# Maxima over two key blocks at once: key differences and relu beside the projections of a two-layer attention and MLP kernel

## The chip, the cores and the metric

The kernel runs on one core of one Trainium2 chip. Its time is what the device takes for one execution, in microseconds (us). The engines of the core work side by side: PE (TensorE) multiplies matrices, DVE (VectorE) and ACT (ScalarE) work on rows of up to 128 partitions, POOL (GpSimd) does the same more slowly and not on PSUM, SP (SyncE) issues DMAs. Each engine runs its own list of instructions in order and waits on the others by semaphores.

## The reference

Two layers, each an attention block and an MLP, on 2048 rows of 640 in fp32:

```python
x = x + _A_ref(_layernorm(x), wqkv, wo)      # 32 heads of 20
x = x + _B_ref(_layernorm(x), w1, b1, w2, b2) # 1536 wide, relu squared
x = x + _A_ref(_layernorm(x), wqkv, wo)
x = x + _B_ref(_layernorm(x), w1, b1, w2, b2)
# _A_ref: q, k, v = heads of x @ wqkv
scores = jnp.einsum("bhqd,bhkd->bhqk", q, k) * (Dh ** -0.5)
p = _softmax(scores, axis=-1)
o = jnp.einsum("bhqk,bhkd->bhqd", p, v)
```

The softmax needs the largest score of every query of every head over all 2048 keys. The kernel computes the scores twice: once with the queries on the partitions, only to take the maxima along the free axis, and once with the keys on the partitions, for the exponentials and the product with v. The negated maxima enter the second product as two more rows of q (against rows of ones in k).

## The kernel before

**Sizes.** Heads go in 8 groups of 4 (`g`), queries in 4 blocks of 512 (`qb`), keys in 4 blocks of 512 (`c`). A block of the attention is `t = 4 g + qb`, 32 in a layer. Matrices are kept as a rounded part and a remainder (`hi`, `lo`), and a product is taken as three.

**A pair.** For one `t`, one key block `c`, one of two head pairs `p` and one 128-row part `sub` of the queries, two matmuls of 60 rows by 512 columns (L434, `by_queries`, one for each head of the pair) give the scores, and DVE takes the maximum of each row. There are 32 × 4 × 8 = 1024 pairs in a layer. The maxima of a `t` lie in one small tile `mx` (`maxima`, 14 buffers), four numbers (one for each `c`) for each head and `sub`; `mrows_max` takes the largest of the four.

**Projections** (`qkv`). 40 units of 15 matmuls (`proj_unit`, L305) give q and k, 16 units of 30 (`v_unit`, L333) give v. The first 16 units make the first two of five row blocks of q and k for all four column blocks `tb`. A unit's result is split on ACT and POOL (`split_on_pool`) or ACT and DVE (`split_to`) and stored to DRAM by SP one unit later (`later`); keys and queries come back from DRAM as tiles of 512 columns, six DMAs each (`rows_of_heads`). After every projection matmul `between` adds 1 (0.65 for v) to a pace, and whenever it reaches 11, `some` issues three pairs (`smax_two`: one L455 reduction over two banks for the two heads). Their results go through three pairs of PSUM banks in turn (`ps_q`). The list of key blocks to work on is `EARLY`: what the finished column blocks allow of group 0, then group 1. The tiles of the next entry are loaded when an entry begins (`tiles`). Key tiles stay in SBUF for later use in `kept`, twelve of them. When all four key blocks of `t = 0` are done, its maxima are turned into rows.

**Attention.** Its order is written out as strings (`ORDERS`): a, b are scores for the exponentials (L502, then ACT's L509), m, n are maxima of the remaining pairs, one head each (L434, then DVE's L446, three banks in turn), V is the product with v of one block of 128 keys for four heads (L514). One string is a turn: 8 V, 32 scores, 12 to 16 pairs. `pairs` picks the string by due time: the remaining pairs, divided over the turns that remain until their block is needed. Finished blocks are divided by their sums on POOL (L558, L569), which waits for DMAs that spread the sums. `begin` loads queries, keys (two groups ahead) and v, and in layer 0 prepares weights on POOL.

**Buffers.** 42 slots of 4 KB a partition (`slot`) hold keys, queries, projections, exponentials and weights; 11 `x` tiles (`xtile`) hold rows, raw weights and the intermediate of the split. A buffer freed in the program goes to the next that asks, who waits until its last reader is done.

Of the kernel before, what the change touches and what calls it, by code (L numbers as in the profile page):

```python
# [28 lines left out]
SLOT = 1024  # L29
HALF = D // 2  # L30
EPS = 1e-5
SCALE = DH ** -0.5
NBLK = NG * NQB
NSLOT = 42
# [4 lines left out]
def tile_layers(  # L39
# [26 lines left out]
    def slot(shape, dtype, label):  # L66
        return arena.tile(shape, dtype, tag="slot", name=name(label))

    def dma(eng, dst, src):

        if dst.dtype == F32R:
            dst = dst.bitcast(F32)
        if src.dtype == F32R:
            src = src.bitcast(F32)
        eng.dma_start(dst, src)  # L75

    def xtile(label):
        return xpool.tile([P, D], F32, tag="x", name=name(label))
# [158 lines left out]
            sp.put(raw, k * 4, k * 4 + 2, 2, eng_hi, eng_lo)  # L237

    d_qk = dram.tile([2, 2, D, S], F32R, name="d_qk")
    d_v = dram.tile([S, H, 32], F32, name="d_v")  # L240
    d_o = dram.tile([D, NQB, 2 * QB], F32R, name="d_o")
    d_one = dram.tile([2, 2, QB], F32R, name="d_one")
# [22 lines left out]
        nc.scalar.copy(dst_hi, src)  # L265
        nc.vector.tensor_sub(dst_lo, src, dst_hi.bitcast(F32))  # L266

    def split_on_pool(dst_hi, dst_lo, src):

        r = xtile("r")[:, :QB]  # L270
        nc.scalar.copy(r, src)  # L271
        pool_hi(dst_hi, r)
        pool_lo(dst_lo, r, dst_hi.bitcast(F32))
# [21 lines left out]


    ORDER = [5, 0, 6, 1, 7, 2, 8, 3, 9, 4]
    xt_ = {}

    def proj_unit(pos, tb, between):  # L300
        dst = ps_pj("pj")
        n = 0
        for k in range(KD):
            for hw, hx in THREE:
                nc.tensor.matmul(  # L305
                    dst,
                    w_qk.piece(pos * 10 + hw * KD + k),
                    xt_[tb][k][:, hx, :],
                    start=(n == 0),
                    stop=(n == 3 * KD - 1),  # L310
                )
                n += 1
                between()
        ev = slot([P, 2, QB], F32R, "ev")
        (split_on_pool if tb or pos > 3 else split_to)(ev[:, 0, :], ev[:, 1, :], dst)
        which, jj = divmod(ORDER[pos], 5)
        return lambda: dma(
            nc.sync,
            d_qk[which, :, jj * P : (jj + 1) * P, tb * QB : (tb + 1) * QB].rearrange(
                "h p t -> p h t"  # L320
            ),
            ev,
        )

    def v_unit(tt, between):
        tb, i = divmod(tt, 4)
# [59 lines left out]
    QSEG = ((0, 0), (DH, 1), (2 * DH, 0))  # L386
    KSEG = ((0, 0), (DH, 0), (2 * DH, 1))

    def rows_of_heads(dst, which, segs, g, b):
        for par in range(2):  # L390
            for off, hl in segs:
                r0 = 64 * par + off
                src = d_qk[which, hl, 4 * g * DH : (4 * g + 4) * DH, b * QB : (b + 1) * QB]
                src = src.rearrange("(a b d) t -> b d a t", a=2, b=2)[par]
                dma(nc.sync, dst[r0 : r0 + DH], src)

    def load_k(g, c, keep):

        if not keep:
            k = slot([P, 2, QB], F32R, "k")  # L400
        elif (g % 3, c) in kept:
            k = kept[g % 3, c]
        else:
            k = kept[g % 3, c] = slot([P, 2, QB], F32R, "k")
# [3 lines left out]
        rows_of_heads(k, 1, KSEG, g, c)  # L408

    def load_q(t):  # L410
        g, qb = divmod(t, NQB)
        q_t[t] = slot([P, 2, QB], F32R, "q")
        rows_of_heads(q_t[t], 0, QSEG, g, qb)

    def load_v(g, c):
        v = slot([P, 8, 4 * 32], F32, "vg")
# [33 lines left out]
    def smax_two(t, p, sub, c):  # L450

        dst = ps_q.two()
        for par in range(2):
            by_queries(dst[:, par, :], t, p, sub, c, par)
        nc.vector.tensor_reduce(  # L455
            maxima(t)[:, 2 * p : 2 * p + 2, sub, c], dst, axis=AX.X, op=ALU.max
        )

    PAIRS = [(p, sub) for p in range(2) for sub in range(4)]

# [121 lines left out]
    def prep_job():  # L582
# [25 lines left out]
    def qkv(first, x_src, rest):  # L608

        pending, groups, work = [], [], []  # L610
        left.update((t, 4) for t in range(NBLK))
        done.clear()
        state = {"pace": 0, "n": 0}
        early, late = {}, {}

        def at(when, n, f):
            when.setdefault(n, []).append(f)
# [30 lines left out]

        def tiles(x):
            g, qb, c = x  # L650
            if (g, c) not in k_t:
                load_k(g, c, True)
            if g * NQB + qb not in q_t:
                load_q(g * NQB + qb)

        def end_group(x):
            g, qb, c = x
            t = g * NQB + qb
            left[t] -= 1
            if left[t]:  # L660
                return
            if t < 1:
                mrows_max(t)
                mrows(t)
                work.append(lambda: mrows_load(t))
            elif t > 2:
                del q_t[t]

        def some(n=3):
            for _ in range(n):  # L670
                if not work:
                    if not groups:
                        return
                    x = groups.pop(0)
                    tiles(x)
                    if groups:
                        tiles(groups[0])
                    work.extend((x, p, sub) for p, sub in PAIRS)
                w = work.pop(0)
                if callable(w):  # L680
                    w()
                    continue
                (g, qb, c), p, sub = w
                smax_two(g * NQB + qb, p, sub, c)
                done.add((g * NQB + qb, p, sub, c))
                if (p, sub) == PAIRS[-1]:
                    end_group(w[0])

        def between(cost):
            state["pace"] += cost  # L690
            if state["pace"] >= 11:
                state["pace"] -= 11
                some()
            state["n"] += 1
            if state["n"] % 4 == 0:
                next(rest, None)

        for n, (tb, pos) in enumerate(UNITS):
            while tb not in xt_:
                next(rest)  # L700
            run(early, n)
            later(proj_unit(pos, tb, lambda: between(1)))
            run(late, n)
            if pos == FIRST - 2:
                tiles(EARLY[tb][0])
            if pos == FIRST - 1:
                groups.extend(EARLY[tb])
            if first:
                w_qk.save_full(1)
                w_v.save_full(1)  # L710
            if pos >= FIRST and tb == NQB - 1 or n == 4 * FIRST - 1:
                w_qk.past(pos * 10 + 9, w_qk.got)
        for tt in range(NKT):
            later(v_unit(tt, lambda: between(0.65)))
            if first:
                w_v.save_full(1)
            if tt % 4 == 3:
                del xt_[tt // 4]
            if tt == 10:
                load_v(0, 0)  # L720
        w_v.drop()
        w_qk.drop()
        later()
        load_v(0, 1)
        while callable((work or [0])[0]):
            some(1)

# [11 lines left out]
    def attention(first, x_src, first_rows):  # L739
# [25 lines left out]
        def begin(i):  # L765

            t, u = divmod(i, NKT)
            g, qb = divmod(t, NQB)
            if u == 1:
                q_t.pop(t - 1, None)  # L770
                if t + 2 < NBLK and t + 2 not in q_t:
                    load_q(t + 2)
            if u % 4 == 1 and qb == 0:
                k_t.pop((g - 1, u // 4), None)
                for h in (1, 2):
                    if g + h < NG and (g + h, u // 4) not in k_t:
                        load_k(g + h, u // 4, True)
                if g and g + 2 >= NG:
                    del kept[(g - 1) % 3, u // 4]
# [12 lines left out]
            if i in split:  # L792
                split.pop(i)()
# [290 lines left out]
```

## Time and profile before

| what | us |
|---|---|
| median of three runs | 3791.23 |
| lowest and highest | 3785.96, 3791.42 |
| profiled execution | 3787.99 |
| its span | 3786.2 |
| projections, layer 0 (18.0 to 335.0) | 317.0 |
| attention, layer 0 (first to last product with v) | 1143.4 |
| projections, layer 1 (1918.0 to 2217.0) | 299.0 |
| attention, layer 1 | 1140.7 |

The profile is one execution. A group's row has the line, the engine, the operation, what it writes and reads with the shape, and its count; behind the bar stand the busy time, the mean in ns of one, and the engine's idle time just before them with what ended it. In a row of windows each engine has its busy time and, in brackets, its count of instructions within the stretch. The chain is the sequence of work that ended last, followed back from the end. P·V matmuls (L514) leave two records each.

### The profile page before, as it was taken

What the parts mean: (1) busy time and instruction counts of PE and PEld (TensorE: products, weight loads), DVE (VectorE), ACT (ScalarE), POOL (GpSimd) and SP (SyncE); (2) the same over time, 40 slices, a digit from 0 to 9 for tenths busy, and PEclk for the clock granted to TensorE, in tenths of its full rate; (3) what the DMA queues carried; (4) which work ended last, traced back from release to release, by engine and by line L of the source; (5) the groups of instructions that cost most, each with busy time, mean ns of one, the idle gap of its engine ahead of it and who ended that gap; (6) DMA issues with size and microseconds to landing.
All of it is one profiled execution on the core that took longest, in us unless ns stands there. A gap on an engine that the chain in (4) does not pass through costs nothing.

```text
span 3786.2 us, 62901 instructions
## 1 busy us (share of the span) xinstructions
PE 3738.8 (99%) x23572; PEld 2135.2 (56%) x23572; DVE 2931.4 (77%) x4500; ACT 2386.3 (63%) x4599; POOL 797.7 (21%) x889
## 2 busy tenths in 40 slices
PE   7999999999999999999999999999999999999999
PEld 5676343444443345988876754444444444369998
DVE  7999999999999993444469999999999999924443
ACT  2114999999999996122211159999999999951221
POOL 5430343211112111111143201211111121201110
PEclk9999999999999999999999999999999999999999
DMA  6553454322121125611244422222232211355111
GB/s 192 176 189 107 135 146 148 108 74 74 48 73 43 35 89 183 239 42 42 89 147 154 166 90 59 67 76 53 65 82 53 60 41 43 102 196 205 42 43 42
DMA packets 243433, 380.81 MB, mean 101 GB/s; under 512 B 65148, under 2 KB 111996, under 8 KB 243128
## 3 DMA queue, kind: packets, MB, share of 16 engines
q1 hardware_dynamic: 242584, 375.08, 32.0%
q8 instruction: 186, 3.05, 0.3%
q10 hardware_dynamic: 544, 1.71, 0.2%
q14 instruction: 119, 0.97, 0.1%
HBM read 244.05 MB, written 132.62 MB: 99 GB/s over the span
## 4 chain that ended last, share of the span: by engine, by line
PE 94%; DVE 3%; DMA 1%; ACT 1%; SPq 0%; issue 0%; POOL 0%; ACTq 0%; DVEq 0%; POOLq 0%
PE banks L514 27%; PE banks L294 20%; PE banks L502 18%; PE banks L434 18%; PE banks L305 6%; PE banks L333 4%; DVE mx L446 1%; DMA k<-d_qk 1%; SPq L75 0%; DVE mx L455 0%; PE banks L914 0%; DMA q<-d_qk 0%; DVE h L266 0%; DVE r L938 0%; ACT e L509 0%
## 5 line engine op out<-in xcount | busy, mean ns | idle before, releaser
L509 ACT ACTIVATE e<-banks 128x512 f32<-128x512 f32 x4096 | 2109.6, 617 | 158.0 <-PE banks L502 96.1
L446 DVE TENSOR_REDUCE mx<-banks 128x1 f32<-128x512 f32 x3204 | 1996.4, 683 | 183.7 <-PE banks L434 134.3
L434 PE MATMUL banks<-k,q 60*128 60x512 f32 x4096 | 1207.6, 443 | 10.8 <-DMA q<-d_qk 8.3
L502 PE MATMUL banks<-q,k 62*128 62x512 f32 x4096 | 1175.4, 430 | 3.1 <-ACT e L509 1.7
L514 PE MATMUL banks<-e,vg 128*32 128x512 f32 x8192 | 1093.0, 605 | 0.0
L434 PEld LDWEIGHTS banks<-k,q 60*128 60x128 f32 x4096 | 578.5, 184 | 636.1 <-DVE mx L446 501.6
L502 PEld LDWEIGHTS banks<-q,k 62*128 62x128 f32 x4096 | 613.8, 185 | 479.9 <-ACT e L509 446.9
L455 DVE TENSOR_REDUCE mx<-banks 128x2 f32<-128x1024 f32 x446 | 518.7, 1220 | 48.9 <-PE banks L434 36.3
L294 PE MATMUL banks<-w,h 128*128 128x320 f32 x2304 | 352.8, 312 | 2.9 <-DVE h L266 2.7
L514 PEld LDWEIGHTS banks<-e,vg 128*32 128x32 f32 x8192 | 161.6, 108 | 341.5 <-issue 319.5
L294 PEld LDWEIGHTS banks<-w,h 128*128 128x128 f32 x2304 | 340.9, 189 | 12.5 <-DVE h L266 6.9
L294 PE MATMUL banks<-xnT,w 128*128 128x512 f32 x1440 | 330.2, 390 | 0.0
L305 PE MATMUL banks<-xnT,wqk 128*128 128x512 f32 x1200 | 309.4, 404 | 0.2 <-DVE ev L266 0.2
L937 ACT ACTIVATE r<-banks,b_t 128x512 f32<-128x512 f32 x96 | 66.1, 688 | 374.9 <-PE banks L294 373.7
L294 PEld LDWEIGHTS banks<-xnT,w 128*128 128x128 f32 x1440 | 269.5, 188 | 55.2
L271 ACT COPY r<-banks 128x512 f32<-128x512 f32 x92 | 53.5, 587 | 341.6 <-PE banks L305 298.6
L305 PEld LDWEIGHTS banks<-xnT,wqk 128*128 128x128 f32 x1200 | 218.4, 190 | 68.7 <-issue 23.7
L558 POOL TENSOR_TENSOR few<-few,minus_t 128x16 f32<-128x16 f32 x62 | 179.9, 2902 | 304.4 <-DMA few<-d_s 299.5
L276 POOL CAST mr<-nt 128x32 fp32r<-128x32 f32 x64 | 13.5, 211 | 976.5 <-DVE nt L474 976.5
L957 DVE TENSOR_TENSOR x<-banks,x 128x320 f32<-128x320 f32 x128 | 62.8, 491 | 200.8 <-PE banks L294 191.5
L569 POOL TENSOR_TENSOR o<-o 128x512 f32<-128x512 f32 x62 | 79.6, 1284 | 553.0 <-PE banks L502 146.3
L938 DVE TENSOR_TENSOR r<-r 128x512 f32<-128x512 f32 x96 | 79.7, 830 | 132.0 <-ACT r L937 131.7
(61 smaller groups left out, 1673.4 us busy)
## 6 DMA issues: line engine op xcount, KB each, us to landing
q<-d_qk SPq DMA_DIRECT2D x636, 80.0 KB
d_qk<-ev SPq DMA_DIRECT2D x80, 512.0 KB
k<-d_qk SPq DMA_DIRECT2D x384, 80.0 KB
x<-d_x SPq DMA_DIRECT2D x96, 320.0 KB
d_o<-ot SPq DMA_DIRECT2D x248, 80.0 KB
ot<-d_o SPq DMA_DIRECT2D x38, 512.0 KB
d_v<-v SPq DMA_DIRECT2D x32, 512.0 KB
vg<-d_v SPq DMA_DIRECT2D x32, 512.0 KB
```

The lines of the kernel that those rows point to most:

```text
L294: nc.tensor.matmul(dst, a, b, start=(n == 0), stop=(n == last))
L305: nc.tensor.matmul(dst, w_qk.piece(pos * 10 + hw * KD + k), xt_[tb][k][:, hx, :], start=(n == 0), stop=(n == 3 * KD - 1),)
L333: nc.tensor.matmul(dst[:, :HALF], xt_[tb][k][:, hx, i * P : (i + 1) * P], w_v.piece(k * 4 + hw * 2 + hf), start=(j == 0), stop=(j == 3 * K ...
L434: nc.tensor.matmul(dst, q_t[t][b : b + 60, p, sub * P : (sub + 1) * P], k_t[t // NQB, c][b : b + 60, p, :], start=True, stop=True,)
L446: nc.vector.tensor_reduce(maxima(t)[:, 2 * p + par, sub, c : c + 1], dst, axis=AX.X, op=ALU.max)
L455: nc.vector.tensor_reduce(maxima(t)[:, 2 * p : 2 * p + 2, sub, c], dst, axis=AX.X, op=ALU.max)
L502: nc.tensor.matmul(dst, k_t[t // NQB, kt // 4][b : b + 62, p, (kt % 4) * P : (kt % 4 + 1) * P], q_t[t][b : b + 62, p, :], start=True, stop ...
L509: nc.scalar.activation(es[p][:, par, :], dst, AF.Exp, scale=SCALE)
L514: nc.tensor.matmul(acc[32 * h : 32 * h + 32, :], v_t[t // NQB, kt // 8][:, kt % 8, 32 * h : 32 * h + 32], es[p][:, par, :], start=(kt == 0 ...
L558: nc.gpsimd.tensor_tensor(few, few, minus_t, op=ALU.pow)
L569: nc.gpsimd.tensor_mul(o[:, 0, :], o[:, 0, :], o[:, 1, :])
L938: nc.vector.tensor_mul(r, r, r)
```

## The change

The maximum over two key blocks A and B is taken at once: with the difference of the keys, D = kB − kA, max(q·kA, q·kB) = q·kA + relu(q·D). So two key blocks still need two matmuls a head, but DVE has one pass over 512 numbers in place of two.

- `proj_unit`: where the unit makes the first two row blocks of k, the copy of even column blocks is kept in a tile `kf`; at odd ones POOL subtracts, splits the difference, and SP stores it to `d_kd`. These eight units always split on POOL.
- `step_two` multiplies with a difference tile and applies relu on ACT into two `x` tiles; `both_two`, one call of `some` later, multiplies with the even block and adds, reduces and stores the maximum in one `tensor_tensor_reduce` a head (two DVE instructions: the pass, and the read of its accumulator). Only columns 0 and 2 of the four are written; so every `mx` tile is first set to −3e38 by POOL.
- 16 of the 128 combinations of group, query block and key block (groups 0 and 1, `qb` 2 and 3, all four `c`) go this way: `DOUBLE`, eight entries, filled in at unit 16. `EARLY` keeps `qb` 0 and 1 of groups 0 and 1 and gains those of group 2.
- `some` runs at a pace of 8.6: three plain pairs, or, while `DOUBLE` lasts, one `both_two`, one plain pair, one `step_two`.
- Sixteen key tiles are kept, and attention loads keys three groups ahead. Keys 1 to 3 of group 0 are dropped when their maxima are done and loaded again beside the v units.

In all, 292 pairs are done beside the projections (128 of them as 64 doubled ones) and 732 in attention.

```diff
-    def rows_of_heads(dst, which, segs, g, b):
+    def rows_of_heads(dst, src_of, segs, g):
...
+    def load_kd(g, x):
+        k_t[g, x] = slot([P, 2, QB], F32R, "kd")
+        rows_of_heads(k_t[g, x], d_kd["de".index(x)], KSEG, g)
...
             mx_t[t] = small.tile([P, 4, 4, 4], F32, tag="mx", bufs=14, name=name("mx"))
+            nc.gpsimd.memset(mx_t[t], LEAST)
...
+        if which and pos < FIRST:
+            if tb % 2 == 0 and jj == 0:
+                keys["of"] = slot([P, 2, QB], F32, "kf")
+            kf = keys["of"][:, jj, :]
+            r = xtile("r")[:, :QB] if tb % 2 else kf
+            split_on_pool(ev[:, 0, :], ev[:, 1, :], dst, r)
+            if tb % 2:
+                kd = slot([P, 2, QB], F32R, "kd")
+                nc.gpsimd.tensor_sub(kf, r, kf)
+                pool_hi(kd[:, 0, :], kf)
+                pool_lo(kd[:, 1, :], kf, kd[:, 0, :].bitcast(F32))
...
+    def step_two(t, p, sub, x):
+        dst = ps_q.two()
+        res = [xtile("rl")[:, :QB] for _ in range(2)]
+        for par in range(2):
+            by_queries(dst[:, par, :], t, p, sub, x, par)
+        for par in range(2):
+            nc.scalar.activation(res[par], dst[:, par, :], AF.Relu)
+        return res
+
+    def both_two(t, p, sub, x, r):
+        dst = ps_q.two()
+        c = 2 * "de".index(x)
+        for par in range(2):
+            by_queries(dst[:, par, :], t, p, sub, c, par)
+        for par in range(2):
+            nc.vector.tensor_tensor_reduce(
+                out=r[par], in0=dst[:, par, :], in1=r[par],
+                scale=1.0, scalar=LEAST, op0=ALU.add, op1=ALU.max,
+                accum_out=maxima(t)[:, 2 * p + par, sub, c : c + 1],
+            )
...
-        [(0, qb, c) for qb in range(NQB) for c in range(NQB) if max(qb, c) == tb]
+        [(0, qb, c) for qb in range(2) for c in range(NQB) if max(qb, c) == tb]
...
-    EARLY[-1] += [(1, qb, c) for qb in range(NQB) for c in range(NQB)]
+    EARLY[-1] += [(1, qb, c) for qb in range(2) for c in range(NQB) if qb + c]
+    EARLY[-1] += [(2, qb, c) for qb in range(2) for c in range(NQB)]
+    DOUBLE = [(g, qb, x) for g in range(2) for qb in (2, 3) for x in "de"]
...
+        def some():
+            while later_rows:
+                mrows_load(later_rows.pop())
+            if not (begun or double or twos):
+                for _ in range(3):
+                    one()
+                return
+            if begun:
+                w, r = begun.pop()
+                (g, qb, x), p, sub = w
+                t = g * NQB + qb
+                both_two(t, p, sub, x, r)
...
+            one()
+            w = following(double, twos)
+            if w:
+                (g, qb, x), p, sub = w
+                begun.append((w, step_two(g * NQB + qb, p, sub, x)))
+            else:
+                one()
...
-            if state["pace"] >= 11:
-                state["pace"] -= 11
+            if state["pace"] >= 8.6:
+                state["pace"] -= 8.6
                 some()
...
+            if n == FIRST + 1:
+                groups.append((1, 0, 0))
+            if n == NQB * FIRST:
+                double.extend(DOUBLE)
...
-                for h in (1, 2):
+                for h in (0, 1, 2, 3):
                     if g + h < NG and (g + h, u // 4) not in k_t:
                         load_k(g + h, u // 4, True)
```

More of the change, by code (lines that the diff above doesn't have):

```diff
@@ L297, in tile_layers @@
     ORDER = [5, 0, 6, 1, 7, 2, 8, 3, 9, 4]
-    xt_ = {}
+    xt_, keys = {}, {}
     def proj_unit(pos, tb, between):
@@ L314, in proj_unit, with store @@
         ev = slot([P, 2, QB], F32R, "ev")
-        (split_on_pool if tb or pos > 3 else split_to)(ev[:, 0, :], ev[:, 1, :], dst)
         which, jj = divmod(ORDER[pos], 5)
[L317 to L323, printed above, removed]
+        rows = slice(jj * P, (jj + 1) * P)
+        kd = None
+        if which and pos < FIRST:
[9 more added lines that the diff above has]
+                pool_lo(kd[:, 1, :], kf, kd[:, 0, :].bitcast(F32))
+                if jj:
+                    del keys["of"]
+        else:
+            (split_on_pool if tb or pos > 3 else split_to)(ev[:, 0, :], ev[:, 1, :], dst)
+        def store():
+            cols = slice(tb * QB, (tb + 1) * QB)
+            dma(nc.sync, d_qk[which, :, rows, cols].rearrange("h p t -> p h t"), ev)
+            if kd is not None:
+                dma(nc.sync, d_kd[tb // 2, :, rows].rearrange("h p t -> p h t"), kd)
+        return store
     def v_unit(tt, between):
@@ L392, in rows_of_heads @@
                 r0 = 64 * par + off
-                src = d_qk[which, hl, 4 * g * DH : (4 * g + 4) * DH, b * QB : (b + 1) * QB]
+                src = src_of[hl, 4 * g * DH : (4 * g + 4) * DH]
                 src = src.rearrange("(a b d) t -> b d a t", a=2, b=2)[par]
@@ L400, in load_k @@
             k = slot([P, 2, QB], F32R, "k")
[L401 to L402 removed]
+        elif (g % 4, c) in kept:
+            k = kept[g % 4, c]
         else:
[L404 removed]
+            k = kept[g % 4, c] = slot([P, 2, QB], F32R, "k")
             for par in range(2):
@@ L407, in load_k @@
         k_t[g, c] = k
-        rows_of_heads(k, 1, KSEG, g, c)
+        rows_of_heads(k, d_qk[1, :, :, c * QB : (c + 1) * QB], KSEG, g)
     def load_q(t):
@@ L457, in smax_two @@
         )
+    def step_two(t, p, sub, x):
[13 more added lines that the diff above has]
+            nc.vector.tensor_tensor_reduce(
+                out=r[par],
+                in0=dst[:, par, :],
+                in1=r[par],
+                scale=1.0,
+                scalar=LEAST,
+                op0=ALU.add,
+                op1=ALU.max,
+                accum_out=maxima(t)[:, 2 * p + par, sub, c : c + 1],
+            )
     PAIRS = [(p, sub) for p in range(2) for sub in range(4)]
@@ L613, in qkv @@
         state = {"pace": 0, "n": 0}
-        early, late = {}, {}
+        early, late, later_rows, ended = {}, {}, [], set()
         def at(when, n, f):
@@ L650, in tiles @@
             g, qb, c = x
-            if (g, c) not in k_t:
-                load_k(g, c, True)
+            for c in [c] if c in range(4) else [c, 2 * "de".index(c)]:
+                if (g, c) not in k_t:
+                    if c in range(4):
+                        load_k(g, c, True)
+                    else:
+                        load_kd(g, c)
             if g * NQB + qb not in q_t:
@@ L658, in end_group, with following, one @@
             t = g * NQB + qb
[L659 to L666, printed above, removed]
-                del q_t[t]
[L669 to L682, printed above, removed]
+            ended.add(x)
+            rest = groups + double
+            if t > 1 and all(y[:2] != (g, qb) for y in rest):
+                del q_t[t]
+            if c not in range(4) and all(y[0] != g or y[2] != c for y in rest):
+                del k_t[g, c]
+            if (
+                g == 0
+                and (0, 2, "d") in ended
+                and all(y[0] for y in rest)
+                and not any(w[0][0] == 0 for w in work + twos + begun)
+            ):
+                for c in range(1, 4):
+                    del k_t[0, c], kept[0, c]
+            if t == 0:
+                left[t] -= 1
+                if left[t] == 0:
+                    mrows_max(t)
+                    mrows(t)
+                    later_rows.append(t)
+        def following(todo, queue):
+            if not queue:
+                if not todo:
+                    return None
+                x = todo.pop(0)
+                tiles(x)
+                if todo:
+                    tiles(todo[0])
+                queue.extend((x, p, sub) for p, sub in PAIRS)
+            return queue.pop(0)
+        def one():
+            w = following(groups, work)
+            if w:
                 (g, qb, c), p, sub = w
@@ L720, in qkv @@
                 load_v(0, 0)
+            if tt == 12:
+                for c in range(4):
+                    if (0, c) not in k_t:
+                        load_k(0, c, True)
         w_v.drop()
@@ L724, in qkv @@
         load_v(0, 1)
-        while callable((work or [0])[0]):
-            some(1)
+        for g, x in [y for y in k_t if y[1] not in range(4)]:
+            del k_t[g, x]
+        assert 0 in done
     ORDERS = {
```

20 lines of the change are left out of this document (15 added, 5 removed).

## The prediction

> **What bounds the kernel now.** I read the page first: engine totals, the slices, the chain that ended last, the costliest groups.
>
> ```profile
> span 3786.2 us, 62901 instructions
> PE 3738.8 (99%) x23572; PEld 2135.2 (56%) x23572; DVE 2931.4 (77%) x4500; ACT 2386.3 (63%) x4599; POOL 797.7 (21%) x889
> PE 94%; DVE 3%; DMA 1%; ACT 1%; SPq 0%; issue 0%; POOL 0%; ACTq 0%; DVEq 0%; POOLq 0%
> L509 ACT ACTIVATE e<-banks 128x512 f32<-128x512 f32 x4096 | 2109.6, 617 | 158.0 <-PE banks L502 96.1
> L446 DVE TENSOR_REDUCE mx<-banks 128x1 f32<-128x512 f32 x3204 | 1996.4, 683 | 183.7 <-PE banks L434 134.3
> L455 DVE TENSOR_REDUCE mx<-banks 128x2 f32<-128x1024 f32 x446 | 518.7, 1220 | 48.9 <-PE banks L434 36.3
> ```
>
> PE is busy nearly everywhere and is 94% of the chain. L455 counts the pairs whose maxima are taken beside the projections: 446, so 223 per layer; L446 counts the rest singly, 3204/2 = 1602, so 801 per layer in attention. Moving a pair does not remove its two matmuls. So the change pays only if a pair costs PE less beside the projections than in attention. Both prices have to be read.
>
> Next the windows by stage, on layer 1 (the second), which is the cleaner one. Columns: stretch, length, then busy time and count of PE, PEld, DVE, ACT, POOL. The first row is eleven turns of the attention's order string, each with 13 pairs; the boundaries are the first P·V matmul of a turn (a turn is 64 P·V records, 32 scores and the maxima, so the counts can be checked).
>
> ```profile
> 2346.99:2543.35 196.36, 196.29 (x1344) 79.40 (x1343) 179.48 (x297) 183.39 (x359) 35.83 (x33) 1.00 0.28 74
> 2310.64:2330.85 20.21, 20.14 (x131) 8.34 (x130) 18.58 (x31) 18.98 (x39) 3.17 (x3) 1.00 0.21 54
> 2330.85:2346.99 16.14, 16.14 (x117) 5.96 (x116) 15.25 (x27) 14.14 (x28) 3.32 (x3) 1.00 0.27 68
> 3260.55:3278.94 18.39, 18.39 (x124) 7.49 (x124) 17.04 (x30) 17.04 (x34) 3.36 (x3) 1.00 0.56 177
> 3278.94:3298.22 19.28, 19.04 (x129) 7.75 (x128) 17.34 (x29) 18.53 (x38) 3.19 (x3) 1.00 0.42 126
> 3298.22:3314.89 16.67, 16.67 (x119) 6.05 (x118) 15.46 (x25) 14.72 (x30) 6.07 (x4) 1.00 0.49 150
> 3331.23:3347.82 16.59, 16.59 (x97) 5.42 (x96) 0.00 (x0) 16.40 (x33) 4.20 (x3) 1.00 0.56 176
> ```
>
> A 13-pair turn takes 196.36/11 = 17.85 us. A 13 followed by a 14 takes 20.21 + 16.14 = 36.35, so the 14 costs 18.50, 0.65 more. A turn with no pair still takes 16.59, and there ACT is busy 16.40 of it: that is the floor.
>
> Last the chain in order of time, in the projections (start, length, what):
>
> ```profile
> 18.37 8.04 PE banks L305 x36
> 40.49 3.49 DVE mx L455 x3
> 46.02 3.40 DVE mx L455 x3
> 282.61 2.69 PE banks L333 x17
> 286.21 2.68 PE banks L333 x17
> 1977.13 2.72 PE banks L305 x11
> 1980.75 2.74 PE banks L305 x11
> ```
>
> Eleven L305 matmuls and a group of three pairs take 3.62 us from start to start. Uninterrupted, L305 runs at 8.04/36 = 0.223 us. Three reduces back to back take 3.40 to 3.49 us, less than 3.62: PE sets this cycle, with DVE close behind.
>
> **Step 1, attention loses 69 pairs per layer.** In the built program of after, 292 pairs stand beside the projections and 732 in attention. The due-time rule then asks for at most 11.95 pairs a turn, so every one of the first 61 turns uses the string of 12; before, they were 13s with five 14s, one 12 and a last 14. The price of a 12 follows from the only full 12 in the trace: 18.39 holds the body of a 13 and the head of the 12, 19.28 the body of the 12 and the head of a 14, 20.21 the body of a 13 and the head of a 14. So head and body of a 12 are 18.39 + 19.28 − 20.21 = 17.46 us: only 0.39 under a 13, not 0.65, since the floor of 16.59 is near. Before, the stretch that these 61 turns replace runs from the first P·V to the 62nd turn: 338.77 to 1434.87 and 2221.44 to 3314.89, 1096.1 and 1093.5 us. After, 61 × 17.46 = 1065. That is −31 and −28.5; layer 0 keeps a slow first turn of about 1 us more, so **−58**. Bounds: 17.85 − 0.65 = 17.20 (−90) and 17.85 (−11). I take 17.46, as it is the string itself.
>
> **Step 2, the projections gain those matmuls.** They are 23 groups of six more in each layer (75 to 98; the pace falls from 11 to 8.6). The three matmul pairs of a group are as before: base, single and difference are all 60-row products. A group costs at least the 0.90 us between the end of one L305 row and the start of the next (3.62 − 2.72), at most 3.62 − 11 × 0.223 = 1.16, counting what the break costs the L305 stream. L333 gives the same: 286.21 − 282.61 = 3.60, less 2.69. I take 1.1, nearer the top, as each new group is a new break: 46 × 1.1 = **+51** (41 to 53). With 58 saved, almost everything is given back here.
>
> **Step 3, DVE and ACT in the doubled cycles.** 64 cycles per layer hold one plain pair (3.45/3 = 1.15 us) and two adding reductions of 512, each with a read of its accumulator as an instruction of its own. Such an operation is not in the trace. The nearest rows:
>
> ```profile
> L266 DVE TENSOR_TENSOR ev<-banks,ev 128x512 fp32r<-128x512 f32 x3 | 2.1, 688 | 6.7 <-ACT ev L265 6.7
> L254 DVE BATCH_NORM_AGGREGATE mv<-bst 128x2 f32<-128x12 f32 x2 | 0.4, 209 | 0.1
> L271 ACT COPY r<-banks 128x512 f32<-128x512 f32 x92 | 53.5, 587 | 341.6 <-PE banks L305 298.6
> L279 POOL TENSOR_TENSOR ev<-r,ev 128x512 fp32r<-128x512 f32 x72 | 92.6, 1286 | 5.8
> L276 POOL CAST ev<-r 128x512 fp32r<-128x512 f32 x72 | 44.1, 613 | 164.5 <-ACT r L271 164.5
> ```
>
> One source in PSUM and one in SBUF: 0.69; the read at most the smallest DVE work, 0.21. So 1.15 + 2 × 0.69 to 0.90 = 2.5 to 2.95 us, against PE's 8.6 × 0.223 + 1.1 = 3.02. PE still sets the cycle: **0**, from −3 to +10; it is the cover that matters, and it is gone when one reduction with its read exceeds (3.02 − 1.15)/2 = 0.93 us. [...] The two relus on ACT are 2 × 0.59 = 1.2 us a cycle; ACT is busy 40.18 of 299 us there, so they hide, and their result is needed only one cycle later.
>
> **Step 4, the plain cycles.** At the head (20 groups by the 16th unit, 14 before) and at the tail (14 groups) the cycles still hold three plain pairs: DVE 3.45 against PE 3.02. In the tail that is 14 × 0.43 = 6, less some 2 that three buffered bank pairs absorb: +4 a layer. In the head the gaps in the list of groups let DVE catch up in layer 1. In layer 0 the normalisations share DVE:
>
> ```profile
> 18.00:92.00 74.00, 64.95 (x295) 46.34 (x294) 54.95 (x85) 17.39 (x32) 45.58 (x62) 0.93 0.55 183
> 1918.00:2217.00 299.00, 294.01 (x1540) 216.76 (x1540) 266.62 (x244) 40.18 (x78) 93.50 (x115) 1.00 0.47 156
> ```
>
> DVE has 19 us free there and 15 pairs × 1.15 = 17 come in; packed imperfectly, +5. Together **+13** (0 to 25).
>
> **Step 5, new waits.** The first difference group begins in the unit where its list is filled, so 6 loads of difference keys and 6 of queries are issued just ahead of the matmul that needs them, on SP behind a store that waits for POOL.
>
> ```profile
> 353.30 2.18 SPq L75 DMA_DIRECT2D k<-d_qk x6
> 1934.98 4.18 DMA q<-d_qk
> PE banks L434 <- DMA q<-d_qk: 4.7, 5, 1.9
> ```
>
> Twelve issues are 2 × 2.18 = 4.4 us, then the landing; SP runs some us ahead of PE. Such waits cost PE at most 1.9 us at a time before (waits of layer 0). I take 4 a layer: **+8** (0 to 16). POOL gets, per layer, four differences (1.29 + 0.61 + 1.29 = 3.2 each) and two more splits of 1.9, 16.6 us in a layer-0 stage where it is busy 45.58 of 74, and a memset of 64 values ahead of every block's first reduction. In attention the memset stands some 10 us of PE work behind POOL's divide or inversion, mostly long enough; beside the projections 1 to 5 us behind a split. A late memset holds DVE, then the banks, then PE: **+6** (0 to 30). Extra loads on SP (16 key tiles kept, four difference tiles, three keys fetched again) lie far ahead of their use: 0. Four fewer free buffers shorten the round of the exp tiles from about 8 units to 7 (15 us), still past the two units that P·V lags: 0.
>
> **Sum**: −58 + 51 + 0 + 13 + 8 + 6 = +20. The profiled execution took 3787.99 us (span 3786.2 and 1.8 around it), 3.2 under the median of 3791.23; so 3808 for a like execution, 3811 as a median. I forecast 3810.
>
> **Rivals.** *Attention gains more* (faster). Place: the 61 turns. If steady 12s run at the PE price, 17.20, the gain is 2 × 61 × 0.26 = 32 more: 3778. For it: PE is 196.29 of 196.36 busy at 13, and 14 costs 0.65 more. Against it: the measured head and body. It decides below 17.23 us a turn, where step 1 exceeds the +78 of the other steps by the 7.6 us that can be told. Chance 0.2.
>
> *The prices cancel.* With 0.90 a group (−9) and half of steps 4 and 5 (−13) the sum is about −2: 3789. Chance 0.15.
>
> *The adding reduction runs at half rate* (slower still). Then 512 columns cost what 1024 do in L455, 1.22, with the read at most 1.43; the cycle is 1.15 + 2.44 to 2.86 = 3.59 to 4.01 on DVE, 0.57 to 0.99 over PE: 128 cycles make +73 to +127, 3883 to 3937. For it: nothing in the trace; against it: L266 reads the same two memories at 0.69. [...] Chance 0.08.
>
> *POOL or DMA in front* (slower): eight memsets a layer late by 2 us each behind splits and inversions, 32, and 8 us instead of 4 at each start of the differences, 8; less the 6 counted already, +34: 3844. For it: POOL's 45.58 of 74 us; against it: the 10 us of cover in attention. Chance 0.12.
>
> That the 292 pairs do not move is excluded by the built order. The forecast itself: 0.45; its own range 3798 to 3828.
>
> **How the numbers follow.** 0.2% (7.6 us) is about what can be told from no change. Faster 0.2 is the first rival; same 0.14 the second; slower 0.66 the rest. The range 3780 to 3858 takes in the first rival's time, a 12 that costs as much as a 13 (+47), and the POOL case; it leaves out the half rate and the far end of the cheap 12s.
>
> **What would show it.** Right: 12-pair turns of 17.4 to 17.6 us; projections longer by 33 to 45 us a layer; adding reductions under 0.75 us with PE still back to back in the doubled cycles. Wrong: turns at 17.2 or under, DVE with PE waiting on it in the doubled cycles, or PE waits behind memsets.

## The result and the profile after

The changed kernel takes 3846.1 us (3843.9 to 3848.2 in four runs) against 3788.6 for the kernel before (four runs as well): a ratio of 1.0153 with an interval of 1.0135 to 1.0170, or 57 us more. The forecast was 3810, +20. The direction was right and the size was not.

The page of after: span, busy times, shares of the chain, and the groups of the maxima.

```profile
span 3846.4 us, 64184 instructions
PE 3735.5 (97%) x23572; PEld 2137.8 (56%) x23572; DVE 2803.9 (73%) x4614; ACT 2522.2 (66%) x4855; POOL 836.2 (22%) x985
PE 87%; DVE 6%; POOL 2%; DMA 2%; SPq 1%; ACT 1%; issue 1%; POOLq 0%; ACTq 0%; DVEq 0%
L473 DVE TENSOR_REDUCE mx<-banks 128x1 f32<-128x512 f32 x2928 | 1841.1, 685 | 248.0 <-PE banks L461 135.6
L482 DVE TENSOR_REDUCE mx<-banks 128x2 f32<-128x1024 f32 x328 | 384.5, 1219 | 49.6 <-PE banks L461 45.7
```

The pairs moved as the change says: L473 (L446 before) has 2928 records, 732 pairs a layer; L482 (L455 before) has 164 plain pairs a layer beside the 128 doubled ones. PE has as many matmuls as before and is busy a little less, 3735.5 against 3738.8, in a span 60 us longer: it stands still for 110.9 us where it did for 47.4. The share of the chain that is not PE rose from 6% to 13%. Standing still is not the whole loss: at a lower clock PE counts as busy too (in a window below for 6.83 of 6.83 us at half clock).

The granted clock fell too. Core, span and mean clock of before and of after:

```profile
core 0: 3786.2 us, clock 0.998
core 0: 3846.4 us, clock 0.985
```

Clock missing from full speed is 0.002 × 3786 = 8 us before and 0.015 × 3846 = 58 us after, each good to 2 us, as the clock is given to 0.001. These 50 us and the pauses overlap in part: in the 6.50 us from 154.20 to 160.70, while PE waits for the loads of the first difference, it is busy for none and the clock stands at 0.50.

By stage, after: both projections, both attentions, then eleven turns of layer 1 with 12 pairs each, a stretch of the doubled cycles, and the tail of the projections.

```profile
18.00:414.00 396.00, 355.13 (x1741) 247.81 (x1743) 302.16 (x483) 125.53 (x242) 142.35 (x184) 0.93 0.49 162
1960.70:2332.20 371.50, 341.64 (x1699) 238.49 (x1697) 280.71 (x442) 111.14 (x213) 111.00 (x141) 0.95 0.46 153
413.77:1525.10 1111.33, 1098.83 (x7599) 437.44 (x7597) 930.05 (x1525) 1063.28 (x2074) 275.69 (x312) 0.99 0.32 94
2332.19:3422.00 1089.81, 1089.70 (x7596) 435.17 (x7597) 930.18 (x1525) 1062.73 (x2074) 204.13 (x208) 1.00 0.25 69
2452.97:2640.54 187.57, 187.57 (x1321) 75.56 (x1320) 167.74 (x275) 183.34 (x359) 36.26 (x38) 1.00 0.27 75
2122.48:2165.52 43.04, 43.04 (x205) 28.59 (x204) 34.30 (x71) 19.49 (x36) 15.35 (x17) 1.00 0.49 166
2281.90:2324.58 42.68, 41.28 (x246) 31.20 (x244) 42.12 (x44) 5.78 (x13) 0.94 (x3) 1.00 0.53 164
```

The same stages of before, projections with all up to the first P·V (layers 0 and 1) and the tail:

```profile
18.00:338.77 320.77, 309.17 (x1599) 226.20 (x1597) 287.03 (x286) 57.86 (x113) 125.51 (x158) 0.98 0.50 169
1917.00:2221.44 304.44, 299.00 (x1565) 219.91 (x1563) 268.92 (x247) 44.15 (x86) 94.50 (x115) 1.00 0.46 155
2181.54:2217.82 36.28, 36.28 (x234) 29.94 (x232) 35.09 (x32) 4.69 (x11) 0.00 (x0) 1.00 0.34 116
```

Attention became shorter by 32 us in layer 0 and 51 in layer 1, 83 in all where 58 were forecast. The projections became longer by 75 and 67, 142 in all where 78 were forecast (steps 2 to 5 and POOL). Both terms were too small, and the second by much more. In the projections the clock is 0.93 and 0.95 where it was 0.98 and 1.00.

**The fill.** One tile's line read as a source: the fill of `mx` on POOL, its time, and who waited for it (us, times).

```profile
L455 POOL MEMSET mx<- x64: 145/152/163, 39.7 to 3308.5; 128x64 f32 x64
  DVE mx L473: 17.3, 6
  DVE rl L503: 6.4, 2
  DVE mx L482: 3.8, 1
```

It takes 0.15 us and DVE waits 27.5 us for it, in 9 places. One of them in layer 0's attention, in order of time, on POOL, DVE and PE (in brackets the idle time before and what ended it):

```profile
594.01 0.72 POOL L279 CAST w<-raw 128x640 fp32r<-128x640 f32 x1 [5.06 <-DMA raw<-in_B_w_dram]
594.81 1.68 POOL L282 TENSOR_TENSOR w<-raw,w 128x128 fp32r<-128x128 f32 x2
596.42 0.15 POOL L455 MEMSET mx<- 128x64 f32 x1
...
596.61 3.68 DVE L473 TENSOR_REDUCE mx<-banks 128x1 f32<-128x512 f32 x6 [5.44 <-POOL mx L455]
...
597.35 0.49 PE L461 MATMUL banks<-k,q 60*128 60x512 f32 x1 [4.14 <-DVE mx L473]
```

POOL waits for a weight's DMA, prepares the weight, and only then comes to the fill, which uses nothing of that weight. DVE waits for the fill, the three banks stay full, and PE stops for 4.14 us. What follows shows in the windows of that turn and of a stretch inside it (the column behind POOL is the granted clock):

```profile
587.71:612.58 24.87, 20.73 (x121) 7.87 (x120) 15.32 (x27) 16.84 (x34) 9.52 (x13) 0.86 0.43 123
597.88:604.71 6.83, 6.83 (x28) 2.33 (x27) 4.63 (x10) 4.24 (x8) 3.90 (x5) 0.50 0.29 69
```

The turn takes 24.87 us where its like take 17.05: 7.8 more. About 4.1 is the pause; the rest, 3.7, is close to half of the 6.83 us in which PE then works at half clock (3.4). PE is busy in all of those 6.83 us, and only in the 7.87 us behind them, to the end of the turn, is the clock 1.00 again.

**The first differences.** The chain in order of time in layer 0's projections, a window of the same place, and PE's waits for query loads, of before and of after (us, times, longest):

```profile
150.52 1.26 POOL ev L282
151.78 0.42 POOL wqk L282
...
152.22 0.34 SPq L76
...
154.03 3.73 DMA kd<-d_kd
...
157.78 4.22 DMA q<-d_qk
```

```profile
154.20:167.80 13.60, 6.32 (x15) 4.02 (x17) 0.00 (x0) 1.19 (x2) 0.00 (x0) 0.50 0.49 118
```

```profile
PE banks L434 <- DMA q<-d_qk: 8.3, 9, 1.9
```

```profile
PE banks L461 <- DMA q<-d_qk: 35.2, 9, 10.5
```

SP's loads stand behind a store that waits for POOL (in layer 0 that of a weight, which POOL prepares behind a split); six difference rows and then six query rows follow, and the last lands 9.8 us after that store was issued. PE waits 35.2 us for queries in the two layers together, up to 10.5 at a time, where it waited 8.3 before; in the window it is busy for 6.32 of 13.60 us, at a clock of 0.50. Behind the wait nine matmuls of L308 take 4.13 us at that clock, 0.46 each, where 36 of the same took 8.04 us at 1.00 in before, 0.22 each. Two places make some 30 of the 35 us: the first difference, and the entry (1, 0, 0), which `groups.append` puts into the list at unit `FIRST + 1`.

### The profile page after: what moved, and what is told of

It is laid out like the page before. It is cut to its first block, busy times and chain, and to the rows that moved or that the text cites. A ratio compares the mean times of both kernels' runs of the same rounds, so it can differ in the third digit from the quotient of the medians.

```text
span 3846.4 us, 64184 instructions
## 1 busy us (share of the span) xinstructions
PE 3735.5 (97%) x23572; PEld 2137.8 (56%) x23572; DVE 2803.9 (73%) x4614; ACT 2522.2 (66%) x4855; POOL 836.2 (22%) x985
## 4 chain that ended last, share of the span: by engine, by line
PE 87%; DVE 6%; POOL 2%; DMA 2%; SPq 1%; ACT 1%; issue 1%; POOLq 0%; ACTq 0%; DVEq 0%
PE banks L569 26%; PE banks L297 20%; PE banks L557 19%; PE banks L461 14%; PE banks L308 5%; DVE mx L482 4%; PE banks L355 3%; SPq L76 1%; DVE x L263 0%; PE banks L1024 0%; DVE bst L255 0%; DMA q<-d_qk 0%; DMA d_qk<-ev 0%; PE banks L385 0%; POOL ev L282 0%
## 5 line engine op out<-in xcount | busy, mean ns | idle before, releaser
L473 DVE TENSOR_REDUCE mx<-banks 128x1 f32<-128x512 f32 x2928 | 1841.1, 685 | 248.0 <-PE banks L461 135.6
L461 PE MATMUL banks<-k,q 60*128 60x512 f32 x3840 | 1184.3, 440 | 50.4 <-DMA q<-d_qk 17.8
L557 PEld LDWEIGHTS banks<-q,k 62*128 62x128 f32 x4096 | 602.4, 186 | 715.8 <-ACT e L564 672.4
L461 PEld LDWEIGHTS banks<-k,q 60*128 60x128 f32 x3840 | 547.4, 187 | 388.8 <-DVE mx L473 219.1
L482 DVE TENSOR_REDUCE mx<-banks 128x2 f32<-128x1024 f32 x328 | 384.5, 1219 | 49.6 <-PE banks L461 45.7
L308 PE MATMUL banks<-xnT,wqk 128*128 128x512 f32 x1200 | 331.9, 421 | 1.7 <-POOL wqk L282 1.7
L493 ACT ACTIVATE rl<-banks 128x512 f32<-128x512 f32 x256 | 139.4, 596 | 215.9 <-PE banks L461 214.3
L308 PEld LDWEIGHTS banks<-xnT,wqk 128*128 128x128 f32 x1200 | 225.5, 198 | 87.8 <-issue 43.2
L503 DVE CUSTOM_DVE_ANT_0 rl<-banks,rl 128x512 f32<-128x512 f32 x256 | 166.7, 689 | 112.1 <-PE banks L461 99.9
L279 POOL CAST mr<-nt 128x32 fp32r<-128x32 f32 x64 | 13.6, 212 | 1032.8 <-DVE nt L529 1032.8
```

What stands on the lines that cost most here:

```text
L308: nc.tensor.matmul(dst, w_qk.piece(pos * 10 + hw * KD + k), xt_[tb][k][:, hx, :], start=(n == 0), stop=(n == 3 * KD - 1),)
L461: nc.tensor.matmul(dst, q_t[t][b : b + 60, p, sub * P : (sub + 1) * P], k_t[t // NQB, c][b : b + 60, p, :], start=True, stop=True,)
L473: nc.vector.tensor_reduce(maxima(t)[:, 2 * p + par, sub, c : c + 1], dst, axis=AX.X, op=ALU.max)
L482: nc.vector.tensor_reduce(maxima(t)[:, 2 * p : 2 * p + 2, sub, c], dst, axis=AX.X, op=ALU.max)
L493: nc.scalar.activation(res[par], dst[:, par, :], AF.Relu)
L503: nc.vector.tensor_tensor_reduce(out=r[par], in0=dst[:, par, :], in1=r[par], scale=1.0, scalar=LEAST, op0=ALU.add, op1=ALU.max, accum_out= ...
```

## The experiments

Theory: the fill behind POOL's waits and the loads issued at their first use make the difference between +20 and +57, each with half clock behind it (0.50 in the two windows above). Rivals: the doubled cycles are bound by DVE or ACT; the due-time rule makes the turns dearer; or the change costs this even without the waits. The kernels below with the fill and the loads edited, alone and together, and with the fill alone share one set of runs of the kernel before (3792.0), the other four a second (3789.9). With the 3788.6 beside after, the kernel before differs by up to 3.4 us from set to set, so differences across sets are good to some 3 us.

**The fill on DVE, and only where columns stay unwritten.**

```diff
-            nc.gpsimd.memset(mx_t[t], LEAST)
+            if t < 8 and t % 4 > 1:
+                nc.vector.memset(mx_t[t], LEAST)
```

> The changed kernel, but the maxima tiles are filled by DVE itself and only for the four blocks whose columns 1 and 3 stay unwritten. Theory (fills queue on POOL behind work that waits for DMAs, DVE waits for the fill, PE for its banks, and the clock falls after each such stall): the 27 us of DVE waits on the fill in the profile of after vanish, nearly all in layer 0's attention; its four turns of 18.8 to 24.9 us become 17.05; 20 to 30 us less, 3816 to 3826. Rival (the added time lies in the doubled cycles themselves): no change, 3846.

3829.1 us, 17 less than after (1.0101 of before, 1.0086 to 1.0116). Layer 0's attention falls from 1111.3 to 1097.6 and has no more turns of over 20 us, and its projections by some 7.5. That is a little less than expected: four turns of 18.3 to 19.8 us remain in layer 0, and in layer 1 PE gained a wait of 3.7 us for the v weights; with what follows it, the stretch from the first to the 309th v matmul takes 78.0 us instead of 71.8. The edit does two things, another engine and fewer fills; which of them helps, this run does not tell.

**The two loads earlier.** The tiles of (1, 0, 0) are asked for one unit, those of the first difference two units ahead.

```diff
+            if n == FIRST:
+                tiles((1, 0, 0))
+            if n == NQB * FIRST - 2:
+                tiles(DOUBLE[0])
```

> The changed kernel, but the tiles of the first difference entry are loaded two units earlier, and those of the entry (1,0,0) one unit earlier. Theory (PE stands before loads issued just ahead of their matmul, 11.0 and 6.7 us at the first difference, 3.4 and 9.7 us at (1,0,0), and runs at half clock after it): 30 to 45 us less, 3801 to 3816. Rival (DMA or SP is full there and the wait only moves): within 8 us of 3846.

3812.2 us, 34 less than after (1.0054, 1.0037 to 1.0071), as expected. PE's waits for queries fall from 35.2 to 7.1 us:

```profile
PE banks L461 <- DMA q<-d_qk: 7.1, 3, 4.9
```

The gain exceeds the 28 us of waits taken away; clock is the likely rest (0.989 over the profiled execution, against 0.985 in after). The rival that the wait only moves falls.

**Both.**

> Both edits. Theory: the two add up, 50 to 75 us less, 3771 to 3796, about the kernel before (3788.6); turns in both layers 17.05 us. Rival: the waits share their cause and the second edit gains nothing, 3801 or more.

3782.3 us in ten runs, 64 less than after, and now faster than before: 0.9975, 0.9966 to 0.9985. Its stages (layer 0, then layer 1):

```profile
17.90:383.90 366.00, 344.27 (x1739) 241.54 (x1737) 302.50 (x486) 125.43 (x241) 141.59 (x174) 0.97 0.52 175
383.92:1476.60 1092.68, 1092.17 (x7597) 434.71 (x7597) 929.85 (x1525) 1062.82 (x2074) 273.85 (x290) 1.00 0.33 96
1913.70:2262.00 348.30, 336.00 (x1697) 236.22 (x1695) 280.09 (x446) 110.97 (x213) 110.40 (x131) 0.98 0.50 163
2262.01:3352.70 1090.69, 1090.69 (x7598) 434.88 (x7597) 929.54 (x1525) 1062.62 (x2074) 202.18 (x186) 1.00 0.25 69
```

Without those waits attention gains 101 us and the projections cost 89: the idea itself is worth some 10 us, and the rival that the change costs this even without the waits falls. The clock is 0.993, so 0.007 × 3777 = 26 us are missing, against 58. The two edits together take off 10 to 13 us more than the sum of each alone (17 and 34); the stages show it in layer 0, 5 us in its projections and 8 in its attention, but which wait hides which wasn't taken apart. The v units of layer 1 are slower than in after, with 2.6 us of waits for the v weights in them (77.4 us from the first to the 309th v matmul).

**The fill alone, in the kernel before.** Nothing else of the change; the fill has no use there.

```diff
             mx_t[t] = small.tile([P, 4, 4, 4], F32, tag="mx", bufs=14, name=name("mx"))
+            nc.gpsimd.memset(mx_t[t], -3.0e38)
```

> The kernel before with nothing but the fill of every maxima tile on POOL added (one part of the change alone). Theory: POOL lags most in layer 0's attention where it prepares weights, so that DVE and PE wait there: 10 to 30 us more, 3799 to 3819. Rival (the 10 us of PE work between POOL's divide and the fill cover it; the stalls in after come from the fewer free buffers): within 4 us of 3788.6.

3844.7 us: 53 more than before (1.0142, 1.0126 to 1.0157), far above what was expected, and as much as the whole change. The fill as a source, and the worst turn of layer 0:

```profile
L429 POOL MEMSET mx<- x64: 145/152/162, 40.1 to 3327.1; 128x64 f32 x64
  DVE mx L447: 45.7, 15
  DVE mx L456: 4.1, 3
```

```profile
662.78:692.84 30.06, 20.45 (x123) 7.82 (x123) 16.34 (x27) 16.67 (x34) 8.40 (x12) 0.83 0.54 158
```

DVE waits 18 times for 64 fills of 0.15 us, 49.8 us in all. Attention is longer by 36.5 us in layer 0 and by 18.0 in layer 1, nearly all in a few turns of 21 to 30 us instead of 17.85; the projections of layer 0 grow by 2.5. The rival that the stalls come from the fewer free buffers falls, as this kernel has as many as before. In after the same fill costs less, and no turn of layer 1's attention is lengthened by it; presumably because with 12 pairs a turn the first reductions of the blocks fall at other points, which was not tried. So fills on POOL cost 53 us in one kernel, and taking them off POOL gains some 17 to 20 in the other.

**Turns of 12 and 14 in place of 13s,** in the kernel before, to see whether turn prices add up, as step 1 took for granted.

```diff
-            n = min(max(round(state["debt"]), 12), 16)
+            n = 14 if state["debt"] >= 13 else 12
```

> The kernel before, its attention made of turns of 12 and 14 pairs in turn instead of 13s. In after a turn of 12 among 12s takes 17.05 us, in before a 12 between a 13 and a 14 came out at 17.46. Theory (the prices do not add: a turn costs more behind one with another string): a 12 and a 14 together take 35.9 us or more, 0.2 over two 13s (35.70), and the run 3790 to 3805. Rival (the price is 17.05 + 18.50 = 35.55 whatever stands beside it, and the 17.46 was the work of those two turns): 30 x 0.15 x 2 = 9 us less, 3775 to 3785.

3801.5 us (1.0031, 1.0021 to 1.0041): 11.5 more. Four turns of layer 1, and four others a little later, where a 12 begins in the other half of its block:

```profile
2357.39:2429.24 71.85, 71.35 (x489) 27.50 (x488) 65.95 (x109) 66.66 (x131) 13.04 (x12) 1.00 0.31 82
2483.64:2554.98 71.34, 71.34 (x490) 27.68 (x489) 65.87 (x109) 66.94 (x131) 13.00 (x12) 1.00 0.34 90
```

A 12 and a 14 take 35.93 (71.85/2) in the first and 35.67 in the second, where two 13s take 35.70, and where 17.05 (a 12 among 12s) and 18.50 would make 35.55. So prices don't add: the pair costs 0.4 or 0.1 us more, by where it falls; the 35.9 that was expected came in the first place only. The attentions are longer by 5.1 and 0.8. The other 2.7 and 2.1 lie nearly all in the hand-off, by which is meant the time from the start of the last v matmul to the first P·V: 6.2 and 5.6 us instead of 3.6. The first turn has another string here, so that 12 matmuls of scores and 6 of maxima stand in it instead of 8 and 2. Attention with its hand-off is then 7.7 and 2.7 us longer.

**A slower pace at the tail,** on top of both. Once the doubled list is done, `some` comes every 11 again in the v units.

```diff
-            if state["pace"] >= 8.6:
-                state["pace"] -= 8.6
+            pace = 8.6 if cost == 1 or begun or double or twos else 11
+            if state["pace"] >= pace:
+                state["pace"] -= pace
```

> Both edits, and the pace is 11 again once the differences are through (tail of the v units). Theory (there three plain pairs are bound by DVE, and its backlog holds the first scores of attention): the last 171 v matmuls take 38 to 39 us and not 42.7, the hand-off 3.6 and not 7.3; six turns of 13 come back, 5 us a layer; together 3 to 8 us less than with both edits alone. Rival (PE has as much to do whatever the pace): no change.

3778.1 us (0.9972, 0.9960 to 0.9983), 4 less than both edits alone; but 2 of these lie between the two sets, and the intervals overlap, so a gain in all is not shown. The stages are clearer. The tail of layer 1, and a turn of 12 with the 13 behind it:

```profile
2209.56:2246.21 36.65, 36.65 (x233) 30.12 (x232) 34.90 (x37) 5.78 (x13) 0.78 (x2) 1.00 0.63 191
2493.35:2510.31 16.96, 16.96 (x121) 6.90 (x120) 14.97 (x27) 16.58 (x33) 3.32 (x3) 1.00 0.25 65
2510.31:2528.73 18.42, 18.41 (x126) 7.54 (x124) 16.66 (x27) 17.26 (x35) 3.19 (x3) 1.00 0.24 62
```

PE is busy throughout the tail and 6.0 us faster than with the quick pace (42.7), more than expected; the hand-off falls from 7.3 to 5.1 and 5.2, less than expected. But six 13s come back in each attention, and one costs 18.42 among 12s, not 17.85.

**The first keys split on DVE,** on top of both, so that the first block doesn't wait for POOL. ACT copies the keys to `kf`.

```diff
-            split_on_pool(ev[:, 0, :], ev[:, 1, :], dst, r)
+            if tb:
+                split_on_pool(ev[:, 0, :], ev[:, 1, :], dst, r)
+            else:
+                split_to(ev[:, 0, :], ev[:, 1, :], dst)
+                nc.scalar.copy(kf, dst)
```

> Both edits, and the keys of the first column block are split on ACT and DVE, as in the kernel before, with one more copy on ACT for the difference. Theory (POOL, which prepares weights and splits there, is late with the first weights and keys): the 62 first projection matmuls of layer 0 take 18 to 20 us and not 25.9, 6 to 8 us less in all. Rival (the wait is for the loads of queries behind it): under 2 us.

3781.2 us (0.9974, 0.9964 to 0.9983): 1.0 less than both edits alone, which can't be told from nothing. Up to the 62nd projection matmul of layer 0 it takes 24.1 us instead of 25.9 (17.5 before the change), not the 18 to 20 expected: a wait for the first queries remains,

```profile
39.57 0.46 PE L466 MATMUL banks<-k,q 60*128 60x512 f32 x1 [2.06 <-DMA q<-d_qk]
```

so the split on POOL was at most 1.8 of the 8.4 us that were added there.

**All four edits.**

> All four edits. If they add: 10 to 16 us under both edits alone, some 0.5 to 0.65% under the kernel before.

3775.9 us (0.9959, 0.9947 to 0.9972 of before), the lowest median: 14 us under before and 70 under after, though its interval overlaps with those of the three versions above that hold both edits. It is 6 us under both edits alone, less than the expected 10 to 16.

## Why the prediction was wrong in size

Two terms of the sum were far too small: the waits for loads (step 5, +8, where taking them away gains 34) and the fill on POOL (+6, where taking it away gains 17). Step 1 was too small the other way. Of the signs of being wrong two came: turns under 17.2 us, and PE waits behind the fill. One reading does not fit its own numbers: the range was said to take in the first rival's time, but 3778 lies under its lower end of 3780.

**Step 1, attention: right in direction, too small.** A 12 among 12s takes 187.57/11 = 17.05 us, not 17.46. I took head and body of a 12 out of three sums in which it stood between a 13 and a 14, as if turn prices added; the turns of 12 and 14 are off from that by 0.1 to 0.4 us, and a 13 behind a 12 by 0.5 (16.96 + 18.42, against 17.05 + 17.85). The 0.41 by which I missed is of that size; that it has this cause is argued. Even the bound of 17.20 was too high. PE is busy in all of the 187.57 us, so a 12 is still a PE turn; the floor of 16.59, where ACT binds, doesn't reach it. Why neighbours of another length cost more stays open. Measured −83 with the stalls of the fill in it, −101 without; forecast −58.

**Step 2, the added groups: right.** In layer 1 without the waits, the last 341 q and k matmuls take 121.8 us against 112.2 before, with 234 matmuls of maxima between them instead of 184, so 8.3 more groups of six: 1.15 each. In layer 0, from the first to the 309th v matmul it takes 71.4 us against 65.4, with 144 instead of 108: 6.0 for 6 groups, 1.0 each. Forecast 1.1.

**Step 3, the doubled cycles: right.** The adding reduction and the read of its accumulator, in after:

```profile
L503 DVE CUSTOM_DVE_ANT_0 rl<-banks,rl 128x512 f32<-128x512 f32 x256 | 166.7, 689 | 112.1 <-PE banks L461 99.9 <-POOL mx L455 6.4 <-ACT wv L171 2.7
L503 DVE DVE_READ_ACCUMULATOR2_ANT mx<- 128x1 f32 x256 | 21.3, 83 | 0.0
```

0.69 as its nearest row, and 0.08 for the read, which no row of before had: 1.15 + 2 × 0.77 = 2.7 us of DVE against 3.02 of PE. In the window 2122.48:2165.52 PE is busy 43.04 of 43.04 and DVE 34.30. The rival of the half rate falls: no run shows such a rate, and with one source in PSUM and one in SBUF the pass took 689 ns.

**Step 4, the plain cycles: the place right, the size low.** The tail is bound by DVE (42.12 of 42.68 us) and takes 6.4 more. The hand-off, which I hadn't counted, grows by 4.0, before and after in layer 1:

```profile
2217.82:2221.44 3.62, 3.18 (x13) 1.37 (x11) 1.32 (x2) 3.08 (x7) 0.00 (x0) 1.00 0.35 145
2324.58:2332.19 7.61, 5.16 (x20) 2.60 (x18) 5.44 (x6) 3.38 (x7) 0.00 (x0) 0.75 0.51 171
```

DVE is busy 5.44 us in it where it was 1.32, and PE stands still for 2.45 where it did for 0.44: DVE's backlog has to drain before attention starts, and with the pause comes half clock (0.75 on the mean of this window; in its last 3.19 us, from 2329.00, PE is busy for 3.18 at 0.50). Three more groups are in these two stretches, two in the tail and one behind the last v matmul; at 1.15 they are 3.4 of step 2. So 6.4 + 4.0 − 3.4 = 7 a layer are left for DVE and the clock behind its pause, not 4. The head costs 7.2 over its one more group in layer 0 and 3.2 in layer 1 (25.9 and 23.1 us to the 62nd matmul in the kernel with both edits, against 17.5 and 18.7, less 1.15), part of it waits for queries. Some 24 in all, forecast 13, just within its 0 to 25.

**Step 5, loads: wrong by far.** Forecast +8 with a bound of 16; taking the two waits away is worth 34. The place was right for the difference group, the mechanism too (issues behind a store that waits for POOL), and SP's lead was not there. Three things were missed. The wait is up to 10.5 us, since the loads of six and six rows and their landing (4.22) come one after another: I had worked out 4.4 us of issues and then taken 4 for all. The entry (1, 0, 0) has the same fault, and the prediction doesn't mention it. And after such a pause PE works at half clock for a while (behind the 4.14 us of the fill for 6.83 us, at 0.50), which I priced at nothing.

**The fill on POOL: wrong.** Forecast +6 together with the splits, bound 30; alone it costs 53 in the kernel before, and its removal gains 17 in after. I took 10 us of PE work as cover, by POOL's busy time; but the fill stands in POOL's order behind instructions that wait for DMAs (5.06 us for a weight, 10.98 us ahead of the division by the sums in the worst turn of the fill alone). Busy time says nothing of such waits. The rival "POOL or DMA in front" named this place and gave 3844, close to the 3846 measured, though by other sizes, so the closeness is luck: eight fills of 2 us a layer where the waits are fewer and longer, and a start of 8 us where it is two starts of up to 10.5.

The sum: the changes of stages make −83 + 142 = +59 where the spans differ by 60; the forecast's −58 + 78 = +20. Step 1 hides 25 to 43 us of the error of step 5 and the fill, so the total looks nearer than its terms were.

## What to carry to other kernels

In the worst turn of the fill alone an instruction of 0.15 us, behind a wait of 10.98 us in its queue, left PE standing for 9.6 of 30.06 us. So price a small instruction on a queue that waits for DMAs by the wait ahead of it, not by its own time or the queue's busy time; put it on the engine that needs its result, or leave it out where its result isn't read. When a work list gets new entries part of the way through, the first of them has no predecessor that loads its tiles: look for every such first entry, and ask for its tiles earlier, by one or two units here. Here a pause of PE cost its length and what was lost at half clock behind it (4.14 us and some 3.4, by an estimate from the 6.83 us at 0.50), so a price has to hold both; and the price of one step of a schedule is taken among steps of its own kind (a 12 took 17.05 us among 12s, where mixed sums had given 17.46).

## What the runs showed of the hardware

I had not expected how dear the clock makes short pauses: a pause of 4.14 us was followed by 6.83 us at a granted clock of 0.50, and around the pause for the first difference the clock stood at 0.50 in a window of 13.6 us. Over the kernel the missing clock rose from 8 to 58 us, of a loss of 57 to 60. With the waits taken away it fell to 26, and 64 us came back; so of what the two waits cost up to half, 32 us, was clock, and the rest PE standing still. How the two overlap was not taken apart.

POOL took 1284 ns for a 128x512 TENSOR_TENSOR (`o<-o`) where DVE took 682 for the same shape, and no row of POOL in the profiles of before and after has a PSUM bank among what it reads or writes.
